# Four heads a unit instead of two: seven tokens a partition and a block-diagonal tile for the keys left over, in an attention and MLP kernel

## The chip, the core and the metric

The kernel runs on one core of a Trainium2 chip. A core has five engines that run side by side and wait for each other through semaphores: PE (TensorE, matmuls), DVE (VectorE), ACT (ScalarE), POOL (GpSimd) and SP (SyncE, which here only issues DMAs). Each takes its instructions strictly in the order in which they were written for it. Sixteen DMA engines move data between the chip's main memory (DRAM) and the on-chip memory (SBUF); PE's results go to PSUM, eight banks of 2 KB on each of 128 partitions.

A matmul takes a stationary operand (`lhsT`, loaded as weights) and streams the columns of a moving operand (`rhs`) past it; both have the contracted dimension on the partitions. The metric is the device time of one execution in microseconds (us), lower is better.

## The reference, cut to what matters

Eight sequences, twelve heads, 448 tokens, 64 values a head. Queries and keys are normalised, attention is computed without a mask, and its result, put together over the heads, goes through a two-layer MLP. All inputs and the output are float32.

```python
q, k, v: (8, 12, 448, 64); g_q, g_k: (64,); w_in: (768, 2048); w_out: (2048, 768)

def rmsnorm(x, g):
    rms = np.sqrt(np.mean(x * x, axis=-1, keepdims=True) + 1e-06)
    return x / rms * g
q_n, k_n = rmsnorm(q, g_q), rmsnorm(k, g_k)
scores = (1 / np.sqrt(64)) * np.matmul(q_n, k_n.transpose(0, 1, 3, 2))
attn = np.exp(scores - max); attn = attn / (sum + 1e-09)      # along the keys
attn_out = np.matmul(attn, v)
x = attn_out.transpose(0, 2, 1, 3).reshape(8 * 448, 768)
h = x @ w_in
return (h * np.clip(h + 3.0, 0.0, 6.0) / 6.0) @ w_out
```

## The kernel before, in words

**Tiling.** Work on attention goes by pairs of heads: 48 pairs P, six to a sequence ("batch" in the code). A pair's q, k and v are loaded with four consecutive tokens on a partition, so 448 tokens lie on 112 partitions, 1 KB in one run for each head (`load`, line 383). `T` is 4 and `TP` is 112.

**Preparation** (`prep`, lines 387 to 430). q and k are squared (ACT, line 396, or POOL, line 398), summed by token (DVE, line 405), turned into 1/rms by a logarithm and an exponential (ACT, lines 410 and 413), and scaled to bfloat16 (`qks`, line 422, POOL, for the first pair DVE). v is converted to bfloat16 with a column of ones beside each token's 64 values (`va`, lines 340, 342 and 346); the ones give the sums of the softmax.

**Transposes** (`trans`). Scores need the 64 values of a head on the partitions. Pairs 0 to 12 are transposed on PE (line 474) and copied out of PSUM; from pair 13 on SP issues a DMA transpose (line 450). The two heads of a pair come to lie on partitions 0 to 63 and 64 to 127 of `T`. The k half is multiplied by the gains on the way (lines 459, 461, 483 and 485).

**Attention.** For each of four key tiles of 112 keys, two score matmuls, one a head, contract over 64 partitions each (line 504, 448 columns), and one exp on ACT covers both heads (line 509, 896 elements a partition). Four such tiles are a pair's probabilities `eT`, transposed as AV needs them: 32 matmuls a pair of 65 columns (line 522) sum into `X`. DVE takes the reciprocals of the sums (line 538) and multiplies (`xn`, line 541). `xn` is transposed to `xT`, on PE for the first two batches (line 557), later by DMA (line 548).

**MLP.** For each batch, 16 groups of six matmuls give 128 of the 2048 inner features each (`h_group`, line 578, in PSUM banks `M`); ACT computes a relu (line 585) and DVE the gate (line 588), which frees the bank. For each 128 tokens, `y_group` sums 16 matmuls into each half of the output (line 609), copies and stores (line 630). The four column blocks of `w_in` and the four of `w_out` are loaded, with a conversion to bfloat16, by eight DMAs that POOL issues (`weights`, lines 644 and 649).

**Order.** `plan.add` only collects operations with what they read and write. `plan.emit` then writes them out in the order of a fixed list of their numbers, `ORDER` (line 74); `WAY` (line 22) gives, by number, which of several engines takes an operation (for squares, for example, POOL or ACT). So both lists together set every engine's queue, and attention of one batch runs among the MLP of the batch before it. The costs and due times that the calls still carry are not used by `emit`.

**PSUM and fillers.** `S0` and `S1` hold scores (two banks each), `X` the AV sums (two), `M0` and `M1` the MLP groups (one each). Matmuls on a tile of zeros (lines 351 and 527: 120 and 72) fill PE while it has no other work early on.

Of the kernel before, what the change touches and what calls it, by code (L numbers as in the profile page):

```python
# [20 lines left out]
PE, ACT, DVE, POOL, SP = "PE", "ACT", "DVE", "POOL", "SP"  # L21
WAY = {
# [10 lines left out]
}  # L33


class Plan:

    def __init__(self):
        self.ops = []
        self.ways = []  # L40
        self.way = {}
        self.last = {}
        self.readers = {}

    def add(self, ways, want, fn, reads=(), writes=(), load=(), since=0.0, half=False):
        i = len(self.ops)
        self.way[i] = WAY.get(i, 0)
        eng, occ, fin = ways[self.way[i]]
# [12 lines left out]
        self.ops.append((eng, occ, fin, want, fn, preds, load, since, half))  # L61
        self.ways.append(ways)
        return i

    def emit(self, order):
        place = {i: n for n, i in enumerate(order)}
        assert len(place) == len(self.ops)
        for i, o in enumerate(self.ops):
            assert all(place[p] < place[i] for p in o[5])
        for i in order:  # L70
            self.ops[i][4](self.ops[i][0])


ORDER = [
# [128 lines left out]
def kernel(  # L203
# [492 lines left out]
    for P in range(NP):  # L696
# [27 lines left out]
        if j < NPAIR - 1:  # L724
            continue
# [48 lines left out]
```

## Time and profile before

| | |
|---|---|
| median of 3 timed runs | 431.22 us (429.11 to 431.24) |
| the profiled execution: span from the first to the last instruction | 428.2 us, the only time that its page gives for it |
| TensorE clock granted | 0.998 of full speed, mean |
| first transpose on PE, first score, first MLP matmul | 8.45, 11.25, 34.15 us |
| last matmul starts | 424.28 us |
| exps of 896 elements | 192, 0.92 us each |
| AV matmuls, score matmuls | 1536, 384 |
| HBM read, written | 50.23 MB, 11.01 MB |
| largest single wait of PE after 42 us | 2.7 us, at 117.59 us |

A line of the profile names the source line (L504), the engine, the operation, the tile written and the tiles read (buffer numbers left out), the shape as partitions x elements, and how many there were. "PEld" is the load of the stationary operand, which overlaps PE. Busy time on PE overlaps too: a matmul of 448 columns is shown as 0.35 us long, although the next one can start long before it ends. "idle before" is how long the engine stood still ahead of those instructions, and what ended it.

### The profile page before, as it was taken

How to read it: one execution, taken by the hardware profiler on the slowest of the kernel's cores; microseconds unless marked ns; L12 is line 12 of the kernel's file. 1: busy time of each engine (PE TensorE's matmuls, PEld its weight loads, DVE VectorE, ACT ScalarE, POOL GpSimd, SP SyncE). 2: the span in 40 equal slices, each digit the busy share in tenths (PEclk: the TensorE clock that was granted, in tenths of full speed). 3: DMA queues.
4: the chain of work that ended last, by engine and by line, in shares of the span. 5: the costliest groups of instructions: out<-in, count | busy, mean ns of one | idle time of the engine just before them, and what ended most of it. 6: DMA issues, size and time to landing. Idle time of an engine off the chain costs nothing.

```text
span 428.2 us, 9877 instructions
## 1 busy us (share of the span) xinstructions
PE 415.2 (97%) x3946; PEld 238.8 (56%) x3946; DVE 223.9 (52%) x422; ACT 285.7 (67%) x512; POOL 175.9 (41%) x195
## 2 busy tenths in 40 slices
PE   6989999999799999999999999999999999999996
PEld 6666555554455555555556555555555555555564
DVE  5887875558555555564756464356323323243211
ACT  5998898689777756877867777778766555143100
POOL 4998994786373436345704525060422100000000
PEclk9999999999999999999999999999999999999999
DMA  7999999997848972677683793756440342000305
GB/s 258 335 242 279 223 239 228 241 292 178 227 102 221 245 199 66 132 189 195 179 243 112 129 282 71 201 113 172 114 87 13 55 87 72 11 2 22 101 26 149
DMA packets 98929, 67.75 MB, mean 158 GB/s; under 512 B 53156, under 2 KB 95428, under 8 KB 98884
## 3 DMA queue, kind: packets, MB, share of 16 engines
q1 hardware_dynamic: 93248, 60.50, 55.1%
q0 software_dynamic: 5248, 6.29, 8.7%
q8 instruction: 31, 0.51, 0.5%
q10 hardware_dynamic: 388, 0.34, 0.3%
q14 instruction: 14, 0.11, 0.1%
HBM read 50.23 MB, written 11.01 MB: 143 GB/s over the span
## 4 chain that ended last, share of the span: by engine, by line
PE 79%; DMA 5%; ACT 3%; SPq 3%; POOL 3%; issue 3%; DVE 2%; ACTq 0%; POOLq 0%
PE M L578 27%; PE M L609 24%; PE X L522 9%; PE S L504 7%; PE S L609 4%; DMA qk<-in_q_dram 3%; ACT eT L509 3%; SPq L383 2%; POOL qks L422 2%; DMA T<-qks 2%; POOL sq L398 2%; PE X L578 1%; PE X L504 1%; PE S L578 1%; PE X L609 1%
## 5 line engine op out<-in xcount | busy, mean ns | idle before, releaser
L578 PE MATMUL M<-xT,w_in_sb 128*128 128x448 bf16 x714 | 159.1, 353 | 2.7 <-DVE gT L588 2.7
L509 ACT ACTIVATE eT<-S 112x896 bf16<-112x896 f32 x168 | 148.7, 915 | 9.4 <-PE S L504 8.5
L609 PE MATMUL M<-w_out_sb,gT 128*128 128x384 bf16 x752 | 136.8, 326 | 0.3 <-DVE gT L588 0.3
L422 POOL TENSOR_TENSOR qks<-qk,rs 112x512 bf16<-112x512 f32 x94 | 96.2, 1043 | 77.6 <-ACT rs L413 37.4
L588 DVE SCALAR_TENSOR_TENSOR gT<-ts,M 128x448 bf16<-128x448 f32 x119 | 73.1, 616 | 91.5 <-ACT ts L585 91.0
L609 PEld LDWEIGHTS <-gT 128*128 128x128 bf16 x912 | 85.0, 98 | 61.1 <-issue 8.4
L585 ACT ACTIVATE ts<-M 128x448 f32<-128x448 f32 x119 | 64.8, 545 | 59.4 <-PE M L578 58.0
L578 PEld LDWEIGHTS <-w_in_sb 128*128 128x128 bf16 x768 | 67.7, 98 | 62.3 <-issue 13.8
L398 POOL TENSOR_TENSOR sq<-qk 112x512 f32<-112x512 f32 x59 | 60.6, 1041 | 57.1 <-DMA qk<-in_k_dram 29.3
L522 PEld LDWEIGHTS <-eT 112*128 112x128 bf16 x1536 | 60.8, 97 | 22.6 <-issue 7.4
L522 PE MATMUL X<-va,eT 112*128 112x65 bf16 x1536 | 67.1, 194 | 0.0
L405 DVE TENSOR_REDUCE ssq<-sq 112x16 f32<-112x1024 f32 (+1 forms) x50 | 58.4, 1171 | 15.7 <-POOL sq L398 13.3
L504 PE MATMUL S<-T 64*128 64x448 bf16 x336 | 50.1, 354 | 1.6 <-ACT eT L509 1.4
L541 DVE TENSOR_TENSOR xn<-X,rd 112x512 bf16<-112x512 f32 x48 | 33.1, 689 | 3.7 <-DMA xT<-xn 2.6
L504 PEld LDWEIGHTS <-T 64*128 64x128 bf16 x384 | 14.0, 94 | 29.4 <-issue 23.8
L509 ACT ACTIVATE eT<-X 112x896 bf16<-112x896 f32 x24 | 22.0, 916 | 11.3 <-PE X L504 11.2
L396 ACT ACTIVATE sq<-qk 112x512 f32<-112x512 f32 x37 | 23.1, 627 | 8.6 <-DMA qk<-in_k_dram 5.5
L344 DVE COPY y<-M 128x384 f32<-128x384 f32 x25 | 13.8, 553 | 24.4 <-PE M L609 24.2
L538 DVE RECIPROCAL rd<-X 112x8 f32<-112x8 f32 x48 | 9.9, 206 | 30.7 <-PE X L522 30.3
L346 POOL CAST va<-vf 112x512 bf16<-112x512 f32 x24 | 14.7, 616 | 22.0 <-PE X L522 13.2
L609 PE MATMUL S<-w_out_sb,gT 128*128 128x384 bf16 (+1 forms) x128 | 23.1, 316 | 0.0
L342 ACT COPY y<-M 128x384 f32<-128x384 f32 x22 | 10.6, 480 | 14.1 <-PE M L609 12.0
(56 smaller groups left out, 184.6 us busy)
## 6 DMA issues: line engine op xcount, KB each, us to landing
qk<-in_q_dram SPq DMA_DIRECT2D x47, 256.0 KB, 4.3
qk<-in_k_dram SPq DMA_DIRECT2D x47, 256.0 KB, 4.4
vf<-in_v_dram SPq DMA_DIRECT2D x47, 256.0 KB, 4.2
w_in_sb<-in_moe_w_in_dram POOLq DMA_DIRECT2D x4, 768.0 KB, 11.4
w_out_sb<-in_moe_w_out_dram POOLq DMA_DIRECT2D x4, 768.0 KB, 10.6
out_dram<-y SPq DMA_DIRECT2D x7, 336.0 KB, 4.1
out_dram<-y SPq DMA_DIRECT2D x8, 288.0 KB, 3.4
out_dram<-y SPq DMA_DIRECT2D x8, 240.0 KB, 4.5
```

Source lines behind the costliest of these rows:

```text
L396: em(nc.scalar.square(out=sq[:, i], in_=x))
L398: em(nc.gpsimd.tensor_tensor(out=sq[:, i], in0=x, in1=x, op=A_MULT))
L405: em(nc.vector.tensor_reduce(out=ssq[:, s].rearrange("p i n -> p (i n)"), in_=sq[:, s].rearrange("p i (n d) -> p (i n) d", d=D), axis=AX_X ...
L422: em((nc.vector if e == DVE else nc.gpsimd).tensor_tensor(out=qks[:, i].rearrange("p t h d -> p h t d"), in0=qk[:, i].rearrange("p h (t d) ...
L504: em(nc.tensor.matmul(out=ps[:, a, 0:S], lhsT=qkT[r, S + t * TP:S + t * TP + 128], rhs=qkT[r, 0:S], start=True, stop=True))
L509: em(nc.scalar.activation(out=eT[:, t, 0:S2].rearrange("p (a s) -> p a s", a=2), in_=ps[0:TP, :, 0:S], func=EXP, bias=0.0, scale=1.0))
L522: em(nc.tensor.matmul(out=X_ps[:, a, i * E1:(i + 1) * E1], lhsT=eT[:, t, c:c + 128], rhs=va[:, a, t, :], start=(t == 0 and i == 0), stop=( ...
L541: em(nc.vector.tensor_tensor(out=xn[:].rearrange("p i a d -> p a i d"), in0=xv[:, :, :, 0:D], in1=rd[:].unsqueeze(3).to_broadcast([TP, 2, ...
L578: em(nc.tensor.matmul(out=ps[:, 0:S], lhsT=w_in_sb[:, kt, f * 128:(f + 1) * 128], rhs=xT[:, kt, :], start=(kt == 0), stop=(kt == NKT - 1)))
L585: em(nc.scalar.activation(out=ts[:], in_=ps[:, 0:S], func=RELU, bias=0.5, scale=1.0 / 6.0))
L588: em(nc.vector.scalar_tensor_tensor(out=gT[:, f, e * S:(e + 1) * S], in0=ts[:], scalar=1.0, in1=ps[:, 0:S], op0=A_MIN, op1=A_MULT))
L609: em(nc.tensor.matmul(out=ps[:, 0:nc0], lhsT=gT[:, f, i * 128:(i + 1) * 128], rhs=w_out_sb[:, f, c0:c0 + nc0], start=(f == 0), stop=(f == ...
```

## The change

The unit of attention is now four heads: two that follow each other (x = 0, 1) and the two six heads further on (r = 0, 1). There are 24 units U, three to a batch.

- **Seven tokens a partition** (`N` = 7, `HP` = 64). A head's 448 tokens lie on 64 partitions, so two heads fill 128, and r is the free dimension: one DMA for the unit's q and one for k, 1,792 B in a run. A batch's v comes in loads of three units (first batch: one and two): tokens 0 to 2 and 4 to 6 of each partition's seven on the two halves of the partitions (`vf`), token 3 apart (`vl`, 256 B in a run).
- **Three full key tiles a head** (`J` = 3): 128 keys each, two tokens of 64 partitions. The scaling writes the k tokens in the order that brings token n next to token n + 4 (columns 0, 2, 4 and 1, 3, 5); token 3 comes last. Two score matmuls, one for each r on its 64 partitions, and one exp for a tile as before.
- **Left-over keys.** The 64 keys of token 3 of the heads r = 0 and r = 1 are copied into a tile `kd` of 128 x 128 that is zero outside its two diagonal blocks. One matmul over all 128 partitions gives both heads' scores for them; one exp covers x = 0 and 1 (`eL`). `av_left` multiplies by `vd`, which is block-diagonal too, 130 columns at a time.
- **Counts, as built**: score matmuls 384 to 288 + 48; exps of 896 elements 192 to 162, and 12 of 448; AV matmuls 1536 to 1152 of 65 columns + 192 of 130; PE transposes 152 to 160; transposes by DMA 71 to 70; loads of q, k and v 144 to 104.
- **First unit by half heads** (`UR` = 1): its loads, squares, sums, scales, transposes, scores and exps are done apart for r = 0 and r = 1.
- **Engines.** Squares may go to DVE too (12 of 50), scales to DVE (35 of 100) and copies to any of three. Transposes on PE for the first 7 units.
- **w_in** is loaded in eight DMAs, by halves of the partitions, since the order of the 768 features follows the new head order. Output tiles hold whole groups of 64 rows, so a store is 64 rows (60 in all, before 60 of uneven size).
- **Fillers**: 81, before 192.
- **Order.** `ORDER` and `WAY` are new throughout; there is nothing left of the cost figures in the code.

The diff, cut to its core:

```diff
 WAY = {
-    63: 2, 65: 1, 68: 1, 78: 2, 83: 1, 90: 2, 94: 1, 101: 2, 126: 1, 132: 2, 156: 1, 157: 1, 163: 2, 187: 1,
...
+    54: 1, 56: 1, 61: 1, 62: 1, 64: 1, 66: 1, 70: 1, 73: 1, 75: 1, 82: 1, 87: 1, 95: 1, 104: 1, 105: 1, 108:
...
 ORDER = [
-    8, 11, 9, 10, 14, 13, 28, 29, 16, 20, 30, 91, 31, 53, 32, 17, 33, 34, 55, 92, 69, 21, 35, 19, 56, 36,
...
+    15, 36, 38, 39, 37, 40, 44, 56, 32, 26, 41, 27, 57, 34, 54, 16, 43, 12, 17, 55, 64, 89, 13, 58, 65, 45,
...
-    NQK, NV, NSQ, NRS, NQS, NVA, NT, NE, NXN, NXT, NTS, NY = 5, 5, 2, 4, 3, 4, 4, 2, 2, 2, 2, 3
+    NQK, NVF, NV, NSQ, NRS, NQS, NVA, NT, NE, NL, NXN, NXT, NTS, NY = 5, 3, 2, 2, 2, 2, 3, 2, 6, 2, 2, 2, 2, 3
...
+    def halves(U):
+        return [(0,), (1,)] if U < UR else [(0, 1)]
+    def load(U, i):
+        b, u = divmod(U, NU)
+        src, dst = (q, k)[i], qk_r[(2 * U + i) % NQK]
+        for rr in halves(U):
+            def fn(_, rr=rr):
+                rows = bass.AP(src.tensor, src[b, 2 * u + rr[0] * HH].offset,
+                               [[N * D, 128], [HH * S * D, len(rr)], [1, N * D]])
+                em(nc.sync.dma_start(out=dst[:, rr[0]:rr[-1] + 1], in_=rows))
...
+            for i, n0, n1, s0, st in [(0, 0, 4, 0, 1), (0, 4, 7, 4, 1), (1, 0, 4, 0, 2), (1, 4, 7, 1, 2)]:
...
+                plan.add(f"sc{l * m}", [POOL, DVE], f_sc,
...
+                    em(nc.sync.dma_start_transpose(
+                        out=dst[:, x].rearrange("c (n p) -> c n p", p=HP),
+                        in_=qks[x * 64:(x + 1) * 64].rearrange("p i n r d -> p (i n r d)")))
...
+                    scaled(e, kd[p, :, r * HP:(r + 1) * HP], ksrc[p, :, SJ:S], how, p)
...
     def score(...):
...
-                    out=ps[:, a, 0:S], lhsT=qkT[r, S + t * TP:S + t * TP + 128], rhs=qkT[r, 0:S],
+                    out=ps[:, r, 0:S], lhsT=t[p, x, S + j * 128:S + (j + 1) * 128], rhs=t[p, x, 0:S],
...
+    def score_left(U):
+        ps, res = sbank()
+        t, kd, eL = T_r[U % NT], kd_r[U % NT], eL_r[U % NL]
+        def f_s(_):
+            for x in range(2):
+                em(nc.tensor.matmul(
+                    out=ps[:, x, 0:S], lhsT=kd[:, x], rhs=t[:, x, 0:S], start=True, stop=True))
+        def f_e(_):
+            em(nc.scalar.activation(out=eL[:, :, 0:S], in_=ps[:, :, 0:S], func=EXP, bias=0.0, scale=1.0))
...
+    def av_left(U, x):
+        eL, vd = eL_r[U % NL], vd_r[U % NVA]
+        def f_av(_):
+            for i in range(T):
+                em(nc.tensor.matmul(
+                    out=X_ps[:, i // 2, (i % 2) * 2 * E1:(i % 2 + 1) * 2 * E1],
+                    lhsT=eL[:, x, i * TP:i * TP + 128], rhs=vd[:, x].rearrange("p r e -> p (r e)"),
+                    start=False, stop=True, skip_group_check=True))
...
-                em(nc.gpsimd.dma_start(
-                    out=w_in_sb[:, :, cols], in_=moe_w_in[:, cols].rearrange("(k p) n -> p k n", p=128)))
+                    em(nc.gpsimd.dma_start(
+                        out=w_in_sb[r * 64:(r + 1) * 64, :, cols],
+                        in_=moe_w_in[:, cols].rearrange("(r k p) n -> r p k n", r=2, p=64)[r]))
```

More of the change, by code (lines that the diff above doesn't have):

```diff
@@ new lines, in load_v, with fn @@
+    def load_v(b, u0, nu, r):
+        n, h = (2 * b + r) % NVF, 2 * u0
+        for half in range(2):
+            def fn(_, half=half):
+                rows = bass.AP(v.tensor, v[b, r * HH + h].offset + half * (J + 1) * D,
+                               [[N * D, 64], [S * D, 2 * nu], [1, J * D]])
+                em(nc.sync.dma_start(out=vf_r[n][half * 64:(half + 1) * 64, h:h + 2 * nu], in_=rows))
+            plan.add(f"ld_v{nu}", [SP], fn, (), [("vf", n, half, u) for u in range(u0, u0 + nu)])
@@ L628, in f_o @@
                     b = 2 * g + e
[L629 removed]
+                    rows = out[b * S:(b + 1) * S, :].rearrange("(p t) n -> t p n", t=N)[t]
                     em((nc.scalar if eng == ACT else nc.sync).dma_start(
[L631 to L637 removed]
@@ L638, in y_group @@
-                c += m
+                        out=rows[:, c0:c0 + nc0], in_=ys[half * 64:(half + 1) * 64, c0:c0 + nc0]))
+                plan.add(f"st{nc0}", [ACT if final and half else SP], f_o,
+                         [("y", yk, n)] if final else [("y", yk, m) for m in range(2)], [])
     def weights():
         for c in range(4):
-            def f_i(_, c=c):
-                cols = slice(c * 512, (c + 1) * 512)
-                em(nc.gpsimd.dma_start(
-                    out=w_in_sb[:, :, cols], in_=moe_w_in[:, cols].rearrange("(k p) n -> p k n", p=128)))
@@ L725 @@
             continue
         b += 1
[L727 to L739 removed]
+        hs, yt = [("h", b - 1, f) for f in range(NFT)], [("y", *z) for z in ys.get(b, [])]
```

601 lines of the change are left out of this document (295 added, 306 removed), and 262 rows, old and new, of tables (ORDER, WAY).

## The prediction, made before the changed kernel had run

> **What bounds the kernel now.** I read the page's totals and slices first, then busy time by stretch, then the order of PE instructions in time. The page, in its parts 1 and 2:
>
> ```profile
> span 428.2 us, 9877 instructions
> PE 415.2 (97%) x3946; PEld 238.8 (56%) x3946; DVE 223.9 (52%) x422; ACT 285.7 (67%) x512; POOL 175.9 (41%) x195
> ```
>
> PE looks full, but this busy time counts overlapping latencies and filler matmuls. What a matmul costs is the distance of starts, which the instructions in time show (start, length, engine, line, operation, count):
>
> ```profile
> 110.64 1.30 PE L578 MATMUL M<-xT,w_in_sb 128*128 128x448 bf16 x6
> 111.77 0.41 PE L522 MATMUL X<-va,eT 112*128 112x65 bf16 x8
> 112.12 0.55 PE L504 MATMUL S<-T 64*128 64x448 bf16 x4
> 112.60 0.74 PE L578 MATMUL M<-xT,w_in_sb 128*128 128x448 bf16 x3
> 113.18 0.65 PE L522 MATMUL X<-va,eT 112*128 112x65 bf16 x16
> 113.67 0.73 PE L578 MATMUL M<-xT,w_in_sb 128*128 128x448 bf16 x3
> 114.33 0.55 PE L504 MATMUL S<-T 64*128 64x448 bf16 x4
> 117.59 2.43 PE L578 MATMUL M<-xT,w_in_sb 128*128 128x448 bf16 x12 [2.71 <-DVE gT L588]
> ```
>
> Six MLP matmuls take 1.13 us, 0.189 each. Sixteen AV matmuls take 0.49, 0.0307 each. Four score matmuls on 64 partitions take 0.48, not 4 x 0.189 = 0.76: two heads on the two halves of the partitions run at once, so a pair costs one matmul (0.19), and 0.10 is left. The eight AV before them take 0.35 instead of 0.25. So each change between the 64-row scores and anything else costs about 0.094. With these spacings and the instruction counts, PE's own work is 145.5 (768 MLP-in) + 145.2 (912 MLP-out: 880 at 0.162, 32 at 0.082) + 37.1 (192 score pairs) + 47.2 (1536 AV) + 7.5 (152 transposes at 0.049) + 17.7 (188 changes) = 400.2 us. The other 28.0 of the span are waits and fillers. The stretches (us; busy and count of PE, PEld, DVE, ACT, POOL; clock; DMA share; GB/s) say where:
>
> ```profile
> 8.45:34.15 25.70, 23.66 (x412) 17.21 (x410) 22.97 (x49) 24.15 (x44) 24.48 (x26) 1.00 1.08 291
> 34.15:41.59 7.44, 7.21 (x113) 4.65 (x112) 5.29 (x11) 6.48 (x13) 6.16 (x7) 1.00 1.03 292
> 68.35:120.00 51.65, 48.94 (x489) 26.53 (x486) 32.08 (x60) 40.55 (x74) 34.46 (x37) 1.00 0.97 230
> 120.00:424.30 304.30, 303.68 (x2597) 170.76 (x2593) 138.23 (x254) 185.70 (x329) 84.67 (x90) 1.00 0.50 124
> ```
>
> ACT, DVE and POOL are all over 89% busy until 34 us: batch 0's attention waits for exps (ACT) and preparation. At 41.59, where the third MLP-in group starts, PE has done 23.2 us of its work: 18.4 lost. From there to the last matmul at 424.3 it loses 382.7 - 377.0 = 5.7, half of it in the hole at 117.59, where the gate (DVE) stood behind a reduction that waited for a late load. The last 3.9 are the final store. So the kernel is bound by ACT and its feeders for 40 us, then by PE's issue.
>
> **The change, part by part.** All against this execution's span of 428.2; the timed runs (median 431.2) lie about 3 above it, and I add the difference to that median.
>
> *Scores and changes.* 384 score matmuls become 288 on 64 rows plus 48 full-height ones for left-over keys. That looks like 48 x 0.189 = 9.1 saved, but the full-height ones don't pair: 138 pairs and 12 singles (first unit) at 0.193 and 48 at 0.189 are 38.0, against 37.1: +0.9 (+0.3 if singles still overlap). The gain is elsewhere: the new order has 61 runs of scores instead of 94 (37 of six matmuls), 122 changes instead of 188: 66 x 0.094 = -6.2.
>
> *AV.* 1536 at 0.0307 become 1152 plus 192 of 130 columns. No row has 130 columns; fillers of 128 are spaced 0.056, 192 columns 0.082. I take 0.057, nearest in size: 46.3, -0.9 (upper end +4.0).
>
> *Transposes on PE* 152 at 0.049 become 160, 112 of them on 128 rows (0.056, as fillers of 128 columns): +1.2.
>
> PE's work is thus 395.2, -5.0. Added up along the new order, 0.8 of it lies before the third MLP-in group and 4.2 after, where it counts in full.
>
> *The head.* ACT, by back-to-back spacings (exp of 896: 0.80; of 448, by the equal-sized relu: 0.42), has 26.8 us before the first relu instead of 30.1: 21 exp tiles for 24, six of them split. The first half-unit goes down the chain load, square, reduce, ln/exp, scale, transpose, copy, score alone; k lands at 3.3 as now and q about 1.0 later; square 0.55, reduction 0.6, ln and exp 0.45, DVE's scaling behind two reductions of the second half until 7.8, transposes 0.4, copies behind them on DVE until 9.6: first exp at 9.9 instead of 11.76. Against that, unit 1's scaling stands on POOL behind a square of 896 elements (1.04 x 896/512 = 1.8), two V casts and two weight issues: about 1.5 of ACT idle. Together -3.3 - 1.9 + 1.5 = -3.7 for the third group's start; following ACT's queue I get 35.0, -6.6 (unit 0's exps and small operations 6.4, to 16.3; unit 1 from 19.6, seven exps and 0.2, to 25.4; unit 2 with a copy, ln and exp 6.2, to 31.6; then its last AV, its transposes and the rest of twelve single MLP matmuls, 3.4). I take -5.0 (ends -7 and 0: nothing gained where DMA, over 100% busy in the second stretch, sets the pace).
>
> The Trainium skill, TensorE: Matmul & The Clock Gate, Part 1, speaks against this: PE's clock is halved by default and freed only after about 3.4 us of sustained work. These two rows of fillers agree, 0.107 apart early and 0.056 after 6.83 us:
>
> ```profile
> 4.47 1.91 PE L351 MATMUL X<-zero_t 128*128 128x128 bf16 x16
> 7.84 0.83 PE L351 MATMUL X<-zero_t 128*128 128x128 bf16 x12
> ```
>
> By that rule, with 81 fillers for 192 and PE idle before the first transposes, the first transposes and scores would run at half speed; the sum would be some 1 to 3 us higher. ACT's chain covers most of that, so I add nothing.
>
> *Weights.* w_in goes in eight partition halves on POOL's queue. What is late next is column block 1: the new order has 5.9 us of PE work between the issue of its second half and the fifth MLP-in group, and 4.5 for block 3. Issue takes 0.9; a whole block landed like this:
>
> ```profile
> w_in_sb<-in_moe_w_in_dram POOLq DMA_DIRECT2D x4, 768.0 KB, 11.4
> T<-qks SPq DMA_TRANSPOSE x35, 3.6
> ```
>
> Half the bytes land between 5.7 and 11.4: a wait from 0.7 to 6.4 at block 1, 2.1 to 7.8 at block 3, less what PE lags anyway (0 at best). I take +2.0 in all, near the lower ends, as the halves overlap each other. The Trainium skill, DMA: Bandwidth & Descriptors, Rules for kernel authors, says partition halves serialize and aren't worth it; its fit (2.0 us + bytes at 436 GB/s, Anatomy of one DMA) gives an estimate of 3.8 for a half (f32 as read), no wait, and a sum 2.0 lower. The trace, 11.4 for what the fit puts at 5.6, is not with it.
>
> *Later stalls.* 5.7 before. Banks M turn over with 1.9 us of PE work (median) between a group's end and the next on its bank, before 2.3; relu 0.545, gate 0.617 and hand-overs need about 1.5. T and rs hold two units as before (four pairs), but come free a unit at a time instead of a pair. Loads carry an eighth fewer bytes, POOL falls by a third. I take +0.8 (ends -4 and +14).
>
> *Hidden.* 21 fewer exp tiles after the head, POOL's squares moved to DVE (12), 56 whole stores, V's short rows: ACT, DVE and POOL are at most 61% busy after 120 us, and DMA 50%. The final store stays 3.9.
>
> Sum: -5.0 - 4.2 + 2.0 + 0.8 = -6.4: span 421.8, median 424.8.
>
> **The rivals.**
> *All waits hidden* (chance 0.22): head -6.6, PE -4.2, no weight wait, stalls as now: -10.8, 420.4. For it: landings of loads ran from 2.6 to 8.3, so short ones exist; against it: DMA is saturated exactly there.
>
> *Weights late* (0.13): block 3 waits its full 7.8 where the forecast has 2.0: 430.6, no change. For it the four landings, 11.0 to 13.1; against it, halves.
>
> *The T chain becomes the bound* (0.17), the slower one. T has two buffers of a unit where it had four of a pair, so unit U+1's two DMA transposes (1.2 each to issue, 2.9 to 7.5 to land) end only some time after unit U-1's last score, and the scalings kd and kt behind them stand in DVE's and ACT's queues in front of gates, relus and exps. At the tightest units the order leaves 4.1 to 4.9 us of PE work; issue and median landing need 4.8. If the 17 such units lose 0.8 each, as the hole of 2.87 shows one late transfer can, that is 13.6: 438.4. From 0.51 a unit on ((6.4 + 2.2)/17) the kernel is slower. Against it: today 35 such transposes cost DVE and ACT 2.9 us of waiting in all.
>
> That fewer score matmuls save no PE time is not a rival, it is in the sum.
>
> **How the numbers follow.** The forecast has 0.48, its own range 421 to 429.5. The range of 418 to 435 leaves out the better half of the first rival and most of the last. About 0.5% (2.2 us) is what measurement can tell from no change. Faster (under 429.1): 0.22 + 0.41 of the forecast's 0.48 + 0.02 = 0.65. Same: 0.05 + 0.08 + 0.02 = 0.15. Slower: the rest, 0.20.
>
> **What would show it.** Changes: PE's scores still 0.19 a pair with about 0.1 on each side, 122 times. Head: first exp near 9.9, third MLP-in group near 36.6 with 22.4 of work done. Weights: PE waiting for w_in DMA around 40 and 54 us. T chain: DVE's kd and kt waiting for DMA T by more than 8 us in all. I am wrong if PE's waits after the third group exceed 14 us, if the 130-column AV cost over 0.08, or if batch 0 isn't over sooner.

## The result: slower by 2.75%

Four executions of the changed kernel have a median of 443.06 us (440.88 to 453.4), four of the kernel before, run beside them, 431.23 (429.11 to 435.8). The ratio is 1.0275, with a 95% interval of 1.0233 to 1.0318: slower, by 11.8 us of the medians, where the prediction had 6.4 us faster. The ratio leaves out the execution of 453.4 us, which is over 1.5% above the fastest of its four. The profile taken with them is of the longest of the four (453.4 us, span 451.6), in which PE stood still for 5.3 us up to 34.5 us and ran at half clock until 39.7; the readings below are therefore of a second profile of the same kernel, with a span of 444.2, unless they say otherwise.

Its page, parts 1 and 4 (busy time by engine; shares of the chain that ended last):

```profile
span 444.2 us, 9138 instructions
PE 413.3 (93%) x3603; PEld 240.2 (54%) x3603; DVE 255.3 (57%) x487; ACT 271.4 (61%) x469; POOL 133.7 (30%) x157
...
PE 60%; DMA 14%; DVE 6%; POOL 6%; issue 5%; SPq 4%; ACT 3%; ACTq 0%; POOLq 0%; DVEq 0%
```

Before, PE held 79% of that chain and DMA 5%. DVE has 31 us more to do than before (255.3 against 223.9), POOL 42 less, ACT 14 less. By stretch (us; busy and count of PE, PEld, DVE, ACT, POOL; clock; DMA share; GB/s), with the same borders as before: first MLP-in group, third MLP-in group, 120 us, last matmul.

```profile
8.45:37.81 29.36, 24.11 (x284) 15.70 (x282) 20.80 (x36) 22.98 (x44) 18.41 (x20) 0.83 0.77 176
37.81:45.57 7.76, 6.92 (x85) 4.17 (x83) 5.93 (x12) 5.74 (x10) 4.81 (x5) 1.00 1.11 255
45.57:120.00 74.43, 66.01 (x623) 37.83 (x622) 55.79 (x100) 51.30 (x93) 44.15 (x44) 1.00 0.96 200
120.00:440.10 320.10, 312.02 (x2578) 178.85 (x2576) 168.78 (x321) 187.05 (x317) 63.15 (x69) 1.00 0.55 121
```

The third MLP-in group starts at 45.57 instead of 41.59. In the first stretch ACT is 78% busy (22.98 of 29.36) where it was 94%, and the clock is 0.83 where it was 1.00. After 120 us PE still has 8 us of plain idleness.

To see where time goes I use one measure for all kernels, *PE's loss*: the time up to a moment less the work of the matmuls begun by then, each at the spacing it has without a wait (0.0965 a 64-row score, 0.189 an MLP-in matmul, in general n columns / 2.4 ns + 2.5 ns, which fits the medians of the changed kernel, 0.189 for 448 columns, 0.162 for 384 and 0.056 for 130; 0.094 a change between 64-row scores and anything else, nothing for fillers). A *wait* below is the part of the distance between two starts that is more than this spacing. PE's work by this measure is 398.1 us before and 392.4 after. The row "forecast" is the prediction's terms put on the row of before: 4.2 less to the third group (5.0 earlier, 0.8 of it less work), then 2.0 for weights and 0.8 for stalls (shared out between the two later columns as the prediction had them by place: weights to the middle one).

| | third group starts | loss to it | from it to 100 us | from 100 us on | all |
|---|---|---|---|---|---|
| before | 41.59 | 19.0 | 0.7 | 6.2 | 26.0 |
| forecast | 36.6 | 14.8 | 2.7 | 7.0 | 24.6 |
| changed | 45.57 | 24.8 | 9.0 | 13.7 | 47.5 |

So the work fell as forecast, and the waits missed it in all three stretches: by 10.0, 6.3 and 6.7 us. The experiments look for their causes.

### The profile page after: what moved, and what is told of

Read it like the earlier page. It is cut to its first block, busy times and chain, and to the rows that moved or that the text cites. A ratio compares the mean times of both kernels' runs of the same rounds, so it can differ in the third digit from the quotient of the medians.

```text
span 451.6 us, 9138 instructions
## 1 busy us (share of the span) xinstructions
PE 418.9 (93%) x3603; PEld 243.5 (54%) x3603; DVE 260.5 (58%) x487; ACT 272.0 (60%) x469; POOL 131.5 (29%) x157
## 4 chain that ended last, share of the span: by engine, by line
PE 67%; DMA 11%; DVE 8%; ACT 4%; issue 3%; POOL 3%; SPq 2%; ACTq 0%; DVEq 0%; POOLq 0%
PE M L645 22%; PE M L676 22%; PE X L578 5%; PE S L676 4%; PE S L540 4%; DMA T<-qks 4%; DVE qks L428 3%; DMA xT<-xn 2%; ACT eT L545 2%; DMA w_in_sb<-in_moe_w_in_dram 2%; PE X L588 2%; PE X L540 2%; DMA vl<-in_v_dram 1%; PE X L645 1%; PE S L559 1%
## 5 line engine op out<-in xcount | busy, mean ns | idle before, releaser
L545 ACT ACTIVATE eT<-S 128x896 bf16<-128x896 f32 (+1 forms) x108 | 92.6, 875 | 15.9 <-PE S L540 15.6
L428 POOL TENSOR_TENSOR qks<-qk,rs 128x512 bf16<-128x512 f32 (+2 forms) x65 | 65.5, 1026 | 85.6 <-ACT rs L417 58.2
L578 PEld LDWEIGHTS <-eT 128*128 128x128 bf16 x1152 | 49.2, 101 | 19.7 <-issue 7.6
L399 POOL TENSOR_TENSOR sq<-qk 128x896 f32<-128x896 f32 x23 | 38.8, 1692 | 67.8 <-DMA qk<-in_k_dram 46.9
L578 PE MATMUL X<-va,eT 128*128 128x65 bf16 x1152 | 52.9, 198 | 3.1 <-POOL va L325 2.5
L404 DVE TENSOR_REDUCE ssq<-sq 128x14 f32<-128x896 f32 (+1 forms) x50 | 51.7, 1039 | 4.0 <-ACT sq L397 3.8
L545 ACT ACTIVATE eT<-X 128x896 bf16<-128x896 f32 x42 | 38.5, 916 | 12.5 <-PE X L540 8.8
L540 PE MATMUL S<-T 64*128 64x448 bf16 x204 | 33.9, 370 | 5.3 <-ACT eT L545 2.4
L428 DVE TENSOR_TENSOR qks<-qk,rs 128x384 bf16<-128x384 f32 (+3 forms) x35 | 33.8, 972 | 2.2 <-DMA T<-qks 1.1
L540 PEld LDWEIGHTS <-T 64*128 64x128 bf16 x288 | 12.3, 94 | 28.7 <-issue 19.7
L323 DVE COPY y<-M 128x384 f32<-128x384 f32 x20 | 11.0, 554 | 24.8 <-PE M L676 20.0
L563 ACT ACTIVATE eL<-S 128x896 bf16<-128x896 f32 x24 | 22.0, 916 | 3.4 <-PE S L559 3.3
```

Source lines behind the costliest of these rows:

```text
L399: em((nc.gpsimd if e == POOL else nc.vector).tensor_tensor(out=o, in0=x, in1=x, op=A_MULT))
L404: em(nc.vector.tensor_reduce(out=ssq[:, i, a * N:z * N], in_=sq[:, a * N * D:z * N * D].rearrange("p (n d) -> p n d", d=D), axis=AX_X, op= ...
L428: em((nc.vector if e == DVE else nc.gpsimd).tensor_tensor(out=qks[:, i, s0:s0 + st * (l - 1) + 1:st, a:z].rearrange("p n r d -> p r n d"), ...
L540: em(nc.tensor.matmul(out=ps[:, r, 0:S], lhsT=t[p, x, S + j * 128:S + (j + 1) * 128], rhs=t[p, x, 0:S], start=True, stop=True))
L545: em(nc.scalar.activation(out=eT[:, a * S:z * S].rearrange("p (r s) -> p r s", s=S), in_=ps[:, a:z, 0:S], func=EXP, bias=0.0, scale=1.0))
L563: em(nc.scalar.activation(out=eL[:, :, 0:S], in_=ps[:, :, 0:S], func=EXP, bias=0.0, scale=1.0))
```

## The experiments

The kernels of the experiments ran in four groups, on three chips, so each is given by its ratio to executions of the kernel before that ran with it (medians of 430.5 to 431.4 us); the changed kernel has 1.0275. PE's loss and the waits are read from the profiled execution of each kernel, whose time can lie some us from the median of all.

### The changed kernel once more

> The changed kernel once more, unaltered, for a profile on the same chip as the runs beside it. Theory A (the scalings and squares that the change moved to DVE are tensor_tensors with two SBUF inputs; each stands still while a POOL instruction runs, and with it DVE's queue of gates, copies and scalings): about 441 us; the 35 DVE scalings at L428 add to 28 us or more, where their unhindered lengths (0.55 for 128x384, 0.68 for 128x512) give about 20; PE's waits over 0.15 us add to 25 or more, and the largest lies between 25 and 36 us behind a DVE scaling. Theory B (the head: half-unit chain, fewer fillers, half clock): the same time, but DVE's scalings close to 20 us in sum and PE's loss before the third MLP-in group made of waits for ACT and of work at half clock.

It took 440.75 to 452.08 us in four executions (median 447.0, the profiled one 445.96, the kernel before 430.88); the mean of all eight executions of the changed kernel is 445.9. PE's waits of over 0.15 us add to 36.5 in the profile, 21.2 of them after the third group (in the kernel before 4.0 there). The scalings on DVE, by shape (count | busy us, mean ns of one | idle before):

```profile
L428 DVE TENSOR_TENSOR qks<-qk,rs 128x384 bf16<-128x384 f32 x20 | 15.7, 789 | 1.0 <-ACT rs L417 0.5 <-DMA T<-qks 0.4
L399 DVE TENSOR_TENSOR sq<-qk 128x896 f32<-128x896 f32 x12 | 13.9, 1159 | 4.9 <-DMA qk<-in_k_dram 4.8
L428 DVE TENSOR_TENSOR qks<-qk,rs 128x512 bf16<-128x512 f32 x11 | 9.5, 861 | 0.0
L428 DVE TENSOR_TENSOR qks<-qk,rs 128x256 bf16<-128x256 f32 x2 | 1.1, 572 | 0.3 <-ACT rs L417 0.3
L428 DVE TENSOR_TENSOR qks<-qk,rs 128x192 bf16<-128x192 f32 x2 | 0.8, 406 | 0.0
```

They add to 27.1 us, just under the 28 of theory A; undisturbed ones (0.55 for 128x384, 0.68 for 128x512) would add to about 20. With the squares, 12 instructions are over 0.15 us too long, by 7.8 us together. But the largest hole between 25 and 36 us, 1.1 us at 28.94, stands behind POOL's va, not behind DVE as theory A had it. In the first profile, of the execution of 453.4 us, it stood behind DVE. These are that profile's lines on DVE, POOL and PE (start, length, engine, line, operation, idle before):

```profile
28.19 0.29 POOL L325 CAST vd<-vl 64x128 bf16<-64x128 f32 x1
28.26 6.20 DVE L428 TENSOR_TENSOR qks<-qk,rs 128x512 bf16<-128x512 f32 x1
...
28.45 1.04 POOL L428 TENSOR_TENSOR qks<-qk,rs 128x512 bf16<-128x512 f32 x1
...
29.43 0.70 POOL L704 DMA_DIRECT2D w_in_sb<-in_moe_w_in_dram  x1
30.13 0.52 POOL L325 CAST va<-vf 128x384 bf16<-128x384 f32 x1
...
30.59 3.31 POOL L399 TENSOR_TENSOR sq<-qk 128x896 f32<-128x896 f32 x2
...
34.52 0.93 PE L489 MATMUL M<-identity,qks 128*128 128x128 bf16 x7 [5.29 <-DVE qks L428]
```

A scaling that takes 0.68 elsewhere takes 6.20: it begins while POOL is at a cast, and ends 0.6 us after POOL's work runs out (33.90). PE waits 5.29 us for it. In that profile 13 DVE instructions are too long, by 13.8 us together. Theory A has its case, though not at every point, and theory B too: ACT is idle in the head and the clock low.

### DVE and POOL by themselves

No attention; six instructions in a row on DVE, POOL or both, from one tile in SBUF, in twelve phases (the core of it):

```diff
+    def scale(e, o, l=4):            # 128x512, two inputs from SBUF
+        e.tensor_tensor(out=..., in0=qk..., in1=rs...to_broadcast([128, 2, l, 64]), op=A_MULT)
...
+    for name, pl, dv in PH:          # C: DVE's scale beside POOL's scale, F: DVE's square, I: its reduce ...
+        for eng, job, tag in ((nc.gpsimd, pl, "p"), (nc.vector, dv, "d")):
+            for _ in range(6):
+                fn(eng, o)
```

> No attention and no MLP: twelve short phases of six instructions each, DVE and POOL alone and side by side, on one tile of q; the output holds zeros. Theory A: side by side with six POOL scalings (each about 1.04 us), DVE's scaling (two SBUF inputs; 0.68 alone) takes 1.0 to 1.8 on average, with single ones of several us, or POOL's are lengthened by as much; its square likewise; the reduction, the copy that also sums (one SBUF input) and the scaling of a PSUM tile keep their lengths to 5%. If the trace's long scalings have another cause, all keep their lengths.

Groups by tile; the tile's first letter is the engine (p POOL, d DVE), the second the phase (A: POOL's scaling, B and E: DVE alone; in C, F, I and J DVE beside POOL's scaling. K's DVE scalings, which read PSUM, ran first, and the last four of them fell beside phase A):

```profile
L56 POOL TENSOR_TENSOR pF<-qk,rs 128x512 bf16<-128x512 f32 x6 | 10.8, 1802 | 7.6 <-DVE qk L98 7.2
L64 DVE TENSOR_TENSOR dF<-qk 128x896 f32<-128x896 f32 x6 | 10.2, 1696 | 0.2
...
L56 POOL TENSOR_TENSOR pC<-qk,rs 128x512 bf16<-128x512 f32 x6 | 8.4, 1402 | 5.2 <-DVE qk L98 4.8
L56 DVE TENSOR_TENSOR dC<-qk,rs 128x512 bf16<-128x512 f32 x6 | 7.8, 1296 | 0.2
L64 DVE TENSOR_TENSOR dE<-qk 128x896 f32<-128x896 f32 x6 | 6.5, 1091 | 0.2
L74 DVE TENSOR_REDUCE dI<-qk 128x14 f32<-128x896 f32 x6 | 6.5, 1086 | 0.2
...
L56 POOL TENSOR_TENSOR pA<-qk,rs 128x512 bf16<-128x512 f32 x6 | 6.3, 1046 | 4.2 <-DMA qk<-in_q_dram 3.8
...
L77 DVE TENSOR_TENSOR dK<-xps,rs 128x512 bf16<-128x512 f32 x6 | 4.1, 692 | 0.9 <-PE xps L52 0.7
L56 DVE TENSOR_TENSOR dB<-qk,rs 128x512 bf16<-128x512 f32 x6 | 4.1, 691 | 0.2
L70 DVE TENSOR_SCALAR_CACHE_REDUCE dJ<-qk 128x384 bf16<-128x384 f32 x6 | 3.3, 553 | 0.2
```

DVE's scaling goes from 0.69 alone to 1.30, and POOL's beside it from 1.05 to 1.40; DVE's square from 1.09 to 1.70 and POOL's scaling beside that to 1.80. The reduction and the summing copy keep 1.09 and 0.55 beside POOL's scaling, and the scalings that read PSUM and one tile of SBUF keep 0.69 on both sides of POOL's start at 4.24. So the cost hangs on two inputs from SBUF on DVE beside a POOL instruction, as theory A has it. The Trainium skill, SBUF — State Buffer, section "Who interferes with whom", states this: a DVE instruction with two SBUF inputs contends with a GpSimd (POOL) instruction that reads SBUF, and one with at most one such input, outside certain fast modes, does not. The runs agree on both. They also show what a turn costs: after the first, each of the DVE scalings in phase C took 1.417, its own 0.691 and 0.726 more, out of the 1.046 that POOL's takes alone. It is POOL's instruction that sets this wait: DVE's square waits 0.726 too (1.091 to 1.817), and beside POOL's square of 1.68, in a phase not shown above, DVE's scaling waits 1.36 (0.691 to 2.05).

### Scalings to POOL, squares to ACT

```diff
+for _i in (104, 167, 168, 221, 223, 384, ..., 1954, 1955, 1956):   # 31 scalings of units 1 to 23
+    WAY[_i] = 0
```

> The changed kernel with the 31 DVE scalings of units 1 to 23 on POOL; the first unit and the order are left. Theory A: the 8 us or more that these scalings took beyond their own length, and the holes on PE behind them, go: 430 to 437 us, ratio to the changed kernel 0.975 to 0.99. Theory B: within 0.5% of the changed kernel, 439 to 443. A third way: POOL (131 us busy, then some 165) is the bound in the first 60 us, where its queue is already without a gap: 445 to 455, with PE waiting for POOL's qks.

Ratio 1.0365 (1.0314 to 1.0415; 444.3 to 448.7 us, beside 440.75 to 452.08 of the changed kernel in the same group): no gain. The hole behind DVE's scaling is not in its profile, but POOL, now 152.7 us busy, is late in the head: PE waits 1.5 us for POOL's qks up to 30.80 and again up to 43.65, and 3.7 for w_in up to 69.48, whose issues stand in POOL's queue. That is the third way of the expectation, in part.

```diff
+for _i in (159, 161, 379, 605, ..., 1901, 1948):   # the 12 squares of DVE
+    WAY[_i] = 1
```

> The changed kernel with the 12 DVE squares on ACT, nothing else. Theory A: each square has two SBUF inputs as well, 13 us of DVE time and what POOL adds to it leave DVE; 1 to 4 us faster, 437 to 440. Theory B: within 1 us. If ACT (272 us busy) is the tighter engine where they lie: 1 to 4 us slower.

Ratio 1.045 (1.0393 to 1.0506; 447.7 to 454.7 us). Its profile has the long scaling at 28.3 us again (5.5 us too long), so the squares don't make it, and ACT's extra 9.5 us of work bought nothing. How much of the slowing is the squares' place on ACT and how much the chance of the long scaling, this run doesn't tell.

### Loads and T transposes left out

```diff
 def load(U, i): ...
+                if U > 2:
+                    return
 def load_v(b, u0, nu, r): ...                     # and load_vl
+                if b > 1:
+                    return
```

> The changed kernel without the q and k loads of units 3 to 23 and the V loads of batches 2 to 7; their instructions work on what the buffers hold, so the output is not the reference's. Theory L (loads of 448 and 288 KB stand late in SP's queue, and POOL, ACT and DVE wait for them in order): 8 us or more faster than the changed kernel (443): 425 to 435, and less than 3 us of waiting on PE after 45 us. If what is left after the head is engines standing behind one another (theory G: reductions, scalings of T and casts of a unit in one piece, in front of gates and relus): 438 to 443.

Ratio 1.0178 (1.0106 to 1.025; 436.4 to 442.8 us, median 438.4): by time this is theory G's range, at its low end, not theory L's. PE's waits after the third group still add to 12.0, where theory L had under 3. Yet PE's loss is 4.6 from the third group to 100 us (9.0 with the loads) and 10.0 behind it (13.7). Why the loads matter is to be read in the chain of work that ended last, of the changed kernel with them (start, us on the chain, what):

```profile
6.49 6.75 DMA vf<-in_v_dram
...
37.17 5.60 DMA vl<-in_v_dram
...
60.41 8.88 DMA w_in_sb<-in_moe_w_in_dram
...
81.80 6.25 DMA qk<-in_k_dram
...
168.58 4.28 DMA vf<-in_v_dram
...
227.69 3.79 DMA qk<-in_k_dram
...
234.73 4.13 DMA qk<-in_k_dram
...
308.66 4.57 DMA vf<-in_v_dram
```

Seven times the end of the kernel hangs on a load of q, k or v (three times, all of q, in the kernel before), and once on w_in: they are issued when their buffer is free and the engine that issues them has come to them, and needed when they land. Part of the gain can come from elsewhere: without the loads a half of w_in lands in 5.3 us instead of 7.5 and a transpose of T in 3.5 instead of 4.2 (medians), and this run doesn't tell the two apart.

```diff
                     def f_d(_, x=x):
+                        if U > 8:
+                            return
                         em(nc.sync.dma_start_transpose(
...
-                scaled(e, dst[p, :, S:S + SJ], ksrc[p, :, 0:SJ], how, p)
+                scaled(e, dst[p, :, S:S + SJ], ksrc[p, :, 0:SJ], how, p, gp_t if U <= 8 else one_t)
```

> The changed kernel without the DMA transposes of T from unit 9 on (30 of 34); kd, kt and the scores read the T of units 7 and 8, kt scales it by one, so the output is not the reference's. Theory T (kd and kt of the next unit wait for the transposes, and gates, relus and exps behind them): 5 us or more faster than the changed kernel, 431 to 438. If the T chain matters only now and then: 441 to 443.

Ratio 1.0341 (1.0286 to 1.0397; 443.6 to 447.4 us). By time it says that T costs nothing. But its profile has the long scaling (6.21 us at 27.77) and a third group at 51.42; behind 100 us PE's loss is 7.1 instead of 13.7. So the time alone can't be read here, and the question went to a later run. In the changed kernel's waits (us in total, times, longest) the transposes stand like this:

```profile
DVE kd L469 <- DMA T<-qks: 10.2, 6, 3.8
...
ACT kd L467 <- DMA T<-qks: 5.9, 4, 3.1
...
ACT T L467 <- DMA T<-qks: 0.3, 1, 0.3
```

16.4 us on DVE and ACT, against 2.9 before. (POOL's scalings, which wait until the transposes have read their buffers, wait less: 10.6 us against 19.7.)

### The head: the first unit whole, and more fillers

```diff
-    UR = 1
+    UR = 0
 ORDER = [ ... ]     # the first unit's operations whole, each where its second half stood
```

> The changed kernel with its first unit whole, as the others: loads of 448 KB, squares, scalings, transposes, copies and exps of both halves in one, each where the second half's stood. If the half-unit brings the first scores forward as the prediction had it: 3 to 6 us slower than the changed kernel, 446 to 449. If it costs as much as it brings (instructions on 64 partitions are as long as on 128, so copies and scalings of T come twice in ACT's and DVE's queues): within 2 us, 441 to 445, first exp later than 13.6, the third MLP-in group no later than 46.5.

Ratio 1.0299 (1.0246 to 1.0353; 443.2 to 445.1 us): the half-unit brings nothing. The first exp starts at 13.94 instead of 13.61, but unit 0's exps are over after 7.5 us instead of 10.6, and the third group starts at 43.25 instead of 45.57 (0.8 us of it less work). ACT's lines of the changed kernel show why:

```profile
8.93 0.94 ACT L397 ACTIVATE sq<-qk 128x896 f32<-128x896 f32 x1
9.78 0.88 ACT L467 ACTIVATE T<-M,gp_t 64x768 bf16<-64x768 bf16 x1
12.69 0.90 ACT L467 ACTIVATE T<-X,gp_t 64x768 bf16<-64x768 bf16 x1 [2.02 <-DVE kd L471]
13.61 0.54 ACT L545 ACTIVATE eT<-S 128x448 bf16<-128x448 f32 x1
14.77 0.54 ACT L545 ACTIVATE eT<-S 128x448 bf16<-128x448 f32 x1 [0.62 <-PE S L540]
```

kt of a half-unit, on 64 partitions, is as long (0.88) as a whole unit's (0.92 at 24.09), so it comes twice; the second stands in front of the first exp, whose score had begun at 12.26.

```diff
     for n in range(NW0):
-        warm(S_r[1][:, 0, 0:128], 4, True, [], [("S", 1, 0)], "warm0")
+        warm(S_r[1][:, 0, 0:128], {1: 16, 2: 10, 3: 10, 6: 16}.get(n, 4), True, [], [("S", 1, 0)], "warm0")
```

> The changed kernel with 36 more filler matmuls ahead of the three longest holes of PE before 15 us (48 KB-free work on zeros, as the others). Theory B (clock): without holes the granted clock is full from some 7 us on instead of half until 11 and from 15 to 25; PE's transposes, scores and AV of the first two units run at 0.056, 0.19 and 0.03 instead of twice that, the third MLP-in group starts 2 to 4 us earlier than 45.6, and the time is 438 to 441. If ACT's queue covers it, as the prediction had it: within 1 us of the changed kernel.

Ratio 1.0365 (1.0298 to 1.0433; 445.6 to 450.8 us). The stretches of the changed kernel (columns as above; the clock is the third number from the end):

```profile
10.00:15.00 5.00, 3.56 (x36) 2.29 (x34) 2.26 (x4) 2.33 (x4) 2.95 (x4) 0.96 1.10 239
15.00:20.00 5.00, 4.11 (x40) 2.61 (x40) 4.92 (x6) 3.60 (x9) 2.40 (x2) 0.50 0.62 131
20.00:25.00 5.00, 4.37 (x42) 2.84 (x40) 2.91 (x4) 4.00 (x11) 3.57 (x6) 0.51 0.68 108
```

For ten us PE runs at half speed and ACT, idle for 1.4 and 1.0 us of the two stretches of five, waits for scores: ACT's queue doesn't cover it. With the fillers two stretches of 3.4 us at half clock are left, from 15.8 and from 26.0, and the third group starts at 44.20, 1.4 us earlier, where theory B had a full clock and 2 to 4. And the 1.4 us are lost again: behind 100 us PE's loss is 16.4 instead of 13.7. So the clock has a part in the head, which the time doesn't show; what all of the half clock costs, this run doesn't tell.

### One input, and the causes together

```diff
-                        em(nc.vector.tensor_tensor(out=o, in0=x, in1=x, op=A_MULT))
+                        em(nc.vector.tensor_scalar(o, x, 1.0, None, max, A_ADD, accum_out=junk_t[:]))
...
-                    em(nc.vector.tensor_tensor(out=qks[...], in0=qk[...], in1=rs[...].to_broadcast(...), op=A_MULT))
+                    em(nc.vector.tensor_scalar(qks[...], qk[...], rs[:, i, a * N:a * N + 1], None, A_MULT, A_ADD,
+                                               accum_out=junk_t[:]))
```

> The changed kernel with DVE's 35 scalings and 12 squares in a form that reads one tensor from SBUF: the scaling multiplies by the partition's first factor (it still waits for rs), the square is a maximum with 1, both also sum. Same engines, same order; the output is not the reference's. Theory A (DVE's two-input instructions stand behind POOL's, 7.8 to 13.8 us in the profiles so far): none of them longer than its own length (0.55, 0.68, 1.09 and 0.08 for the sum) by 0.15, no hole of 5 us near 30 us in any execution, 4 to 8 us faster than the changed kernel (441 to 446): 434 to 440. If loads and T set the pace anyway: 441 to 446.

```profile
L432 DVE TENSOR_SCALAR_CACHE_REDUCE qks<-qk,rs 128x384 bf16<-128x384 f32 x20 | 12.1, 606 | 2.4 <-DMA T<-qks 1.1 <-ACT rs L420 0.9
L432 DVE TENSOR_SCALAR_CACHE_REDUCE qks<-qk,rs 128x512 bf16<-128x512 f32 x11 | 8.2, 742 | 0.3
```

The scalings keep to their own length (0.61 and 0.74 in this form), POOL's too (1.05 for 128x512, 1.13 in the first profile), PE waits 1.3 us for DVE's gates and copies (gT and y) in the banks M instead of 6.3, and PE's loss falls from 47.5 to 40.0 in the profiled execution, the fastest of the four. The times fall less: ratio 1.0245 (1.0187 to 1.0304; 438.5 to 444.4 us), by 1.3 us, which is inside what the other view expected and not theory A's 4 to 8, and less than the two intervals leave open. But 1.0275 is without the one of its four executions that is known to have the scaling of 6.20 us. The mean of all eight executions of the changed kernel, 445.9, is 4.3 us above the mean of these four, 441.6. So the price of the two-input forms by themselves lies somewhere between too little to tell from noise and some 4 us.

> The changed kernel without the later loads and without the later DMA transposes of T, as each was left out alone before. If the two waits add up (alone they took 4.3 + 3.6 and 6.7 us off PE's loss after 45 us): 428 to 434. If each only hides the other: 436 to 440, as without loads alone.

Edits as above. Ratio 1.0098 (1.0068 to 1.0127), median 435.45: 7.6 us less than the changed kernel's ratio, 3.4 less than without loads alone. The median lies between the two expectations: of the 14.6 us that the two alone took off PE's loss behind the third group, 12.0 are gone here, so they add up in the main.

> All together: no later loads, no later DMA transposes of T, one-input forms on DVE, 36 more fillers. If these four are what the forecast missed, its work term shows: 421 to 428, with w_in's wait and the first unit's preparation left. If it stays above 432, a cause is missing (theory G: longer instructions of a unit in order on DVE and ACT).

Ratio 0.9949 (0.9926 to 0.9972), 427.3 to 429.5 us, just above the 421 to 428 expected and clear of 432, so theory G isn't needed behind the third group. The four together give back 14.0 of the 18.2 us by which the forecast missed. PE's loss is 21.5 to the third group, 5.4 to 100 us, 3.2 behind it. So the four are enough to account for what the forecast missed behind the third group (9.7 forecast there, 22.7 in the changed kernel, 8.6 here), though leaving loads out also takes away waits that the kernel before had. Of the 10.0 missed in the head, only 3.3 are gone.

The other way round, in the kernel before:

```diff
-            plan.add([(DVE, 1.0, 1.1) if P == 0 else pool(n, 1.95e-3)], want + 0.01, f_sc,
+            plan.add([(DVE, 1.0, 1.1) if P == 0 or (P, i) in ON_DVE else pool(n, 1.95e-3)], want + 0.01, f_sc,
```

> The kernel before with 31 of its 94 POOL scalings (112x512) on DVE, as many in each group of four heads as the changed kernel has; nothing else. Theory A: these run beside POOL's squares and scalings, take 0.9 or more on average (0.68 alone), and hold gates and copies: 3 to 10 us slower than before, 434 to 441. If DVE's in-order queue has room for them: within 1.5 us of before, 430 to 432.5.

```profile
L424 DVE TENSOR_TENSOR qks<-qk,rs 112x512 bf16<-112x512 f32 x33 | 30.3, 925 | 2.1 <-ACT rs L415 1.4 <-DMA T<-qks 0.6
```

Ratio 1.0094 (1.0061 to 1.0127), 433.7 to 436.5 us: 31 scalings moved from POOL to DVE cost the old kernel 4.1 us, and take 0.925 each. This is the cleanest price of the step in a whole kernel: one edit, nothing left out. It is the price of the move, not of standing still alone: the 33 scalings fill 30.3 us of DVE's queue, some 8 of them beyond the undisturbed 0.68 each, and no run parts the two.

### What is left, and the shares

> As the run with everything out (no later loads, no later T transposes, one-input forms, fillers; 428.4), with the first unit whole. If the half-unit's instructions are what is left of the head: unit 0's exps take 7.5 instead of 9.7 us, the third MLP-in group starts 1.5 to 3 us earlier than 42.3, and the time is 425 to 427. If something behind it (preparation of unit 1, batch 0's V) sets the start anyway: 428 to 429.

Ratio 0.9909 (0.9881 to 0.9937), 426.4 to 428.5 us: 1.7 us faster than with the half-unit (by the ratios), as the expectation had it in time but not in place: unit 0's exps take 7.1 us, yet the third group starts only 0.4 earlier, at 41.89. Its waits over 0.15 us behind the third group add to 6.6.

> One-input forms on DVE (441.7 alone) and no DMA transposes of T from unit 9 on. Theory T: 4 to 7 us faster than one-input forms alone, 434 to 438, nearly all of it after 100 us. If T costs only where loads delay it: within 2 us of 441.7.

Ratio 1.0139 (1.0078 to 1.02), 435.1 to 438.8 us: 4.6 us less than one-input forms alone, and the loss behind 100 us is 5.2 instead of 9.6. Theory T holds where the long scaling is out of the way, and the run without loads and T agrees: there too T takes 4.4 us off the loss behind 100 us (10.0 to 5.6).

> One-input forms on DVE and no later loads. Theory L: 5 to 8 us faster than one-input forms alone, 433 to 437, half of it between 45 and 100 us. If the loads' gain was that of the undisturbed DVE: within 2 us of 441.7.

Ratio 1.001 (0.9987 to 1.0033), 428.8 to 432.3 us: 10.1 us less than one-input forms alone, more than expected.

> Complete kernel: the changed one with the first unit whole and 36 more fillers. If the head's gain is kept to the end: 2 to 4 us faster than the changed kernel, 438 to 441. If the waits behind it take it back, as in the two runs alone (443.9 and 446.0): 442 to 446.

Ratio 1.0523 (1.0459 to 1.0587), 445.5 to 455.6 us, three of the four longer than both expectations had it. The profile is of the shortest, 445.5; what made the others 451.7 to 455.6 isn't known. In the profile the third group starts at 43.13, 2.4 us earlier, and the loss behind 100 us is 15.4 instead of 13.7; PE waits 3.3 us for V's cast at 47.95 and 2.2 for w_in at 66.88. The head's gain is not kept.

| left out or changed | ratio to before | loss to third group | to 100 us | from 100 us |
|---|---|---|---|---|
| nothing | 1.0275 | 24.8 | 9.0 | 13.7 |
| one-input forms | 1.0245 | 22.3 | 8.1 | 9.6 |
| loads | 1.0178 | 24.5 | 4.6 | 10.0 |
| one-input, T | 1.0139 | 23.5 | 8.1 | 5.2 |
| loads, T | 1.0098 | 24.0 | 5.1 | 5.6 |
| one-input, loads | 1.0010 | 22.5 | 5.2 | 4.6 |
| one-input, loads, T, fillers | 0.9949 | 21.5 | 5.4 | 3.2 |
| the same, first unit whole | 0.9909 | 21.9 | 5.5 | 3.4 |

Whether the causes add isn't settled. By the ratios, one-input forms alone give 0.30 points, loads alone 0.97, both 2.65, but most of these ratios are known only to half a point, and 1.0275 is without the longest execution. By PE's loss the two do add: 7.5 alone, 8.4 alone, 15.2 together. No complete kernel here beats the kernel before, and even the last row, which leaves work out, is only 0.9% under it: nothing here points to a version of this change worth having.

## Why the prediction was wrong

*PE's work (-5.0): right.* The spacings came out as taken: a score pair 0.19, a change 0.094, 122 of them, the 130-column AV 0.056 (taken 0.057). The work fell from 398.1 to 392.4. The two runs with most of the waits out end at 426.9 and 428.5, near the forecast of 424.8; since they leave out work of other engines too, they are no test of this term by itself.

*The head (-5.0): wrong, 10.0 us of loss too little.* The step that failed is "following ACT's queue". First exp: 13.61, not 9.9; the two kt of a half-unit (0.88 and 0.90) were not in the chain, nor was ACT's square of the next unit (0.94) in front of the first, and the transposes ran slowly (seven in 0.95 us). Unit 0's exps: 10.6 us, not 6.4, while PE and ACT waited for each other in turns and PE ran at half speed (9.7 with the fillers). Unit 1: 7.2, not 5.8; unit 2: 6.9, not 6.2; the rest 5.1, not 3.4. The prediction set no bound for how long a half-unit's instructions stand in these queues, and a copy on 64 partitions takes as long as one on 128. The sentence "ACT's chain covers most of that, so I add nothing" failed with it. The Trainium skill's rule of the clock (TensorE: Matmul & The Clock Gate, Part 1), which I set aside, was the better guide to the state: the clock was at half from 14.7 to 24.9. The fillers took a third of that away (6.8 us at half clock instead of 10.2) and brought 1.4 us at the third group and nothing at the end of the kernel. All this says where the time went; what would bring it back is mostly open. One-input forms and fillers bring 3.3 of the 10.0, a whole first unit nothing more (21.9), and the 21.5 that stay are still above the 19.0 of the kernel before.

*Weights (+2.0): right in size, partly by luck.* PE waits 1.8 us for w_in up to 69.33 (2.4 in the first profile), in block 3, and none in block 1; a half landed in 7.5 (median), inside the bounds of 5.7 to 11.4. But the half of block 3 landed in 8.9, and PE came to it 7.1 us after its issue, where the prediction had 4.5 of work: two misses that nearly cancel.

*Later stalls (+0.8, ends -4 and +14): mis-sized.* From the third group on the loss is 22.7 against 7.0 before: +15.7, or +13.9 without w_in, at the upper end, where the term had +0.8. The prediction's own bound, 14 us of waits behind the third group, is exceeded: 21.2.

*Hidden: wrong, and incomplete.* "POOL's squares moved to DVE (12)" was costed at nothing because ACT, DVE and POOL were at most 61% busy after 120 us, and the 33 scalings that moved with them have no term at all. A share of busy time doesn't show that two engines keep each other out. The trace of before could have shown it: its only two DVE scalings, of one shape, took 0.68 and 1.16, the longer one beside a POOL square.

```profile
6.47 0.68 DVE L422 TENSOR_TENSOR qks<-qk,rs 112x512 bf16<-112x512 f32 x1
...
8.12 1.04 POOL L398 TENSOR_TENSOR sq<-qk 112x512 f32<-112x512 f32 x1
...
8.55 1.16 DVE L422 TENSOR_TENSOR qks<-qk,rs 112x512 bf16<-112x512 f32 x1
```

In the old kernel 31 of these moves cost 4.1 us; in the changed one the two-input forms cost 1.3 us by the ratios and 4.3 by the means of all executions, and 7.2 when loads are out (1.0178 to 1.0010).

*The T chain, the slower rival (0.17): its mechanism is there.* Its sign was waits for T of over 8 us on DVE; there are 10.2, and 6.2 on ACT. Its price is a third of what the rival gave: 4.6 us by the run without T, where the rival had 13.6. At that price it would not have made the kernel slower by itself: for that the rival needed 8.6.

*Loads.* "Loads carry an eighth fewer bytes" was taken as a reason for fewer stalls. They come in pieces of 448 and 288 KB where there were 256; with them out, 4.2 us less (1.0178), and 10.1 less when DVE is undisturbed. No run leaves them out of the kernel before, so how much of this came with the change isn't measured; not all of it is old, for the loads alone make 8.1 us of PE's loss behind the third group, and the kernel before lost 7.0 there in all. That the buffers' depth makes them late is only argued; no run has deeper buffers.

Left open: whether the causes' gains depend on each other, and what else keeps the head at 21.5 us of loss with everything done to it.

## What to carry to other kernels

Before work is moved to an idle engine, look at what its instructions share with those of the engine they leave: in these runs a DVE instruction with two inputs in SBUF and a POOL instruction that reads SBUF took turns (0.69 became 1.42), whatever the busy shares say, and the in-order queue behind the one that waits pays. Halving a unit by partitions doesn't halve the length of its copies (0.88 on 64 partitions, 0.92 on 128), it doubles their number; a head built on that must be priced instruction by instruction, with the clock that its holes leave. Here the saving in PE's work came as forecast and was small (5.7 us), and what PE lost in waits and at half clock (21.5 us more than before) decided the result.

## What the runs showed beyond what I expected

A DVE instruction can be kept out for far more than one POOL instruction. Alone with POOL they took turns, one for one; in the kernel one scaling stood through five POOL instructions and a DMA issue, without a gap between them, 6.20 us instead of 0.68, in three of the nine profiles in which units 1 and 2 had their scalings on DVE in the two-input form and their squares and casts on POOL, and in none of the five with one-input forms. What decides between the two isn't known from these runs.

This may be part of why the time of the changed kernel spreads: 440.8 to 453.4 us in eight executions, against 438.5 to 444.4 in four with one-input forms and 428.8 to 432.3 in ten with one-input forms and without loads. Of the eight only two were profiled, so it isn't shown. The lower mean clock of the longer one of these two (0.974 against 0.988) is a matter of its own stretches at half clock: it has the one of ten us in the head that the other has too, and three more of 3.4 to 6.8, the longest from 32.9 to 39.7, which begins inside the hole that ended at 34.5.
